# Chunk totals of decays by small DMAs, odd positions' sums on VectorE, joined outputs of pair units

## The chip, the cores and the metric

The kernel runs on one core of a Trainium2 chip. The metric is the device time in microseconds of one launch, given as the median of several runs. A core has five engines with a queue of instructions each: TensorE (PE; its weight loads are shown as PEld), VectorE (DVE), ScalarE (ACT), GpSimd (POOL) and SyncE (SP), which here only issues transfers. Each queue is worked off in its order; engines wait for each other through semaphores. Matmuls write PSUM, eight banks of 128 partitions x 512 f32; everything else works on SBUF, 128 partitions wide.

## What is computed

A recurrent attention with decays, then a feed-forward block (FFN) with exact gelu over its output. There are 4 sequences of 768 tokens, 8 heads of 48; the FFN goes from 384 to 2048 and back.

```python
    f = 1.0 / (1.0 + np.exp(-f_logit))
    for t in range(S):
        state = f[:, :, t, :, None] * state + np.einsum('bhd,bhe->bhde', k[:, :, t], v[:, :, t])
        y[:, :, t] = np.einsum('bhd,bhde->bhe', q[:, :, t], state)
    ...
    x = np.ascontiguousarray(attn_out.transpose(0, 2, 1, 3)).reshape(B * S, H * D)
    h = x @ w_in
    g = 0.5 * h * (1.0 + erf(h * inv_sqrt2))
    return (g @ w_out).astype(np.float32)
```

## The kernel before

**Chunks and units.** The 3072 tokens are cut into 24 chunks of 128, six to a sequence, and two chunks make a unit: units 0 to 11. Inside a chunk the recurrence becomes matrix products: with the running sums g of the log decays, k is scaled by exp(-g) (tile `rg`), q by exp(g) (tile `gt`); scores are masked and applied to v, and a state is carried from chunk to chunk. The state has two heads per matrix, so a chunk has four head pairs (`P2`).

**Pair units.** Units 0 to 4 (`PAIRS`) load two neighbouring tokens into one partition. The 256 tokens of such a unit are split by even and odd position j, and each tile's partitions 0 to 63 are the first chunk, 64 to 127 the second. The other units (natural ones) have one chunk per tile.

**Decays.** `decays(u)` takes the log of the forget gates in two ScalarE operations (E at line 478, L at 481: tile `lf`, bf16). A triangular matmul sums them over the tokens: line 494 for a natural chunk; lines 499 and 500 for each position of a pair unit, even and odd. The sums land in a PSUM bank. Two exponentials on ScalarE make `rg` (509) and `gt` (511). The chunk's total decay, which the state needs with the head dimension on the partitions rather than along the row, comes from narrow matmuls with `lf` as the stationary operand: four of one column for a natural chunk (496, against `negcol`), eight of two columns for a pair unit (504, against `negp`), followed by a small exponential into `gl` (514 or 518). Line 524 scales k and q into `sc`; line 529 casts v.

**Scores and state.** `turn` transposes `sc` into `kq`, for units 0 to 3 by TensorE (557, 563), from unit 4 on by a DMA transpose on SP's queue (545). Scores are matmuls (661 natural, 723 pair) masked by VectorE (570). `carry` adds the chunk's outer product to the state (`rr`, 594) and multiplies by the total decay (`tn`, POOL at 596; for the first chunk of a sequence VectorE at 590), then casts the state to bf16 (`sb`, 601). `gl` is read at 590 and 596 only.

**Outputs.** A natural chunk's output is one TensorE run: `inter` (638, with the state) and the products with v (697). In a pair unit the run is split: `intra` (765, in the array's 64-row form, operation `YI`) for both chunks, and for each chunk a separate operation `YX` with the state (`interp`, 644, in a 64-column form). `outputs` copies the result to `yb` (614) and turns it into `xT`, by TensorE in units 0 to 4 (630, 633), by a DMA transpose from unit 5 (618).

**FFN.** A group of two chunks has eight runs of six matmuls, F1 (801), a gelu each (811), and per chunk four runs of four matmuls, F2 (820). The result is copied to `osb` (834) and stored by SP (836). The last chunk's copy is split in halves between ScalarE and VectorE (827), each half stored from the queue of its own (829).

**What sets the order.** `Plan` holds every operation with an estimated duration, what it reads and writes, buffers from small pools (`slots`) and a priority. `Plan.run` places them one by one, always the one that could start earliest, by priority among near ties; the result is each engine's queue, SP's and POOL's included. Priorities get a random term: one draw for all (`SEED`) and one per unit (`SEEDS`), half-width 0.5, 1, 3 or 8 by the seed modulo 4. ScalarE's tables for exponentials and gelu exclude each other; line 865 loads a table where the order changes from one to the other. While TensorE would stand idle in the first 30 us, junk matmuls (859) are put in.

**Loads.** SP issues the loads of f, k, q and v (433 pair units, 441 natural ones) in a fixed order as buffers come free; POOL issues the weights' (445, 448). SP's one queue also holds the DMA transposes and the stores; an instruction there that waits holds back all behind it.

Of the kernel before, what the change touches and what calls it, by code (L numbers as in the profile page):

```python
# [9 lines left out]
F32 = mybir.dt.float32  # L10
BF16 = mybir.dt.bfloat16
AF = mybir.ActivationFunctionType
# [15 lines left out]
SEEDS = [0, 684, 383, 3363, 2427, 131, 74, 3619, 3555, 1021, 519, 3174]  # L28
# [53 lines left out]
class Plan:  # L82
# [30 lines left out]
    def run(self):  # L113
# [4 lines left out]
        for o in self.ops:  # L118
            if o.prio > -5:
                k = min(max(int(o.prio % 1000) // 20, 0), len(SEEDS) - 1)  # L120
                o.prio += rng.uniform(-SPREAD, SPREAD)
                if SEEDS[k]:
                    w = (0.5, 1.0, 3.0, 8.0)[SEEDS[k] % 4]
                    o.prio += own[k].uniform(-w, w)
        act, switched, mode = None, 0.0, 0
# [79 lines left out]

SIZES = [2, 2, 2, 2, 2, 2, 2, 2, 2, 2, 2, 2]
PAIRS = [0, 1, 2, 3, 4]
WIN = [1024, 512, 512]
EG = [0, 1]
# [14 lines left out]
NGT = 4  # L224
WARM = 30.0
# [5 lines left out]
def kernel(  # L231
# [54 lines left out]
    s_gl = slots(6, [C, 2, P2], F32, "gl")  # L286
    s_kq = slots(3, [C, 2, P2, 2, C], BF16, "kq")
# [53 lines left out]
    for i in range(3):  # L341
        P.add("DVE", 0.2, lambda i=i: nc.vector.memset(
            s_sb.tiles[i].rearrange("p a b -> p (a b)").bitcast(F32), 0.0), wr=[f"sbz{i}"], prio=-70)
    z_lf = [f"lfz{i}" for i in range(3)]
# [106 lines left out]
    def decays(u):  # L451
# [32 lines left out]
        gps = [(s_fh if u in EG else s_m).new() for _ in range(2)]  # L484
        for j, n in enumerate(ns):
            y = X[n]
            gt, rg = s_gt.new(), s_rg.new()
            y.update(sc=s_sc.new(), vb=s_vb.new())
            pr = 20 * u + 10 * j

            def cum(j=j, g=gps[j]):
                g = g.t()
                if not pair:
                    nc.tensor.matmul(g[:, 0:HD], trin, lf.t()[:, j, :, 0:D], start=True, stop=True)  # L494
                    for p in range(P2):
                        nc.tensor.matmul(g[:, HD + p:HD + p + 1], lf.t()[:, j, 2 * p:2 * p + 2, :], negcol,  # L496
                                         start=True, stop=True, skip_group_check=True)
                    return
                nc.tensor.matmul(g[:, 0:HD], trip[:, 0, :], lf.t()[:, 0, :, 0:D], start=True, stop=False)
                nc.tensor.matmul(g[:, 0:HD], trip[:, 1 - j, :], lf.t()[:, 1, :, 0:D], start=False, stop=True)  # L500
                if j:
                    for i in range(2):
                        for p in range(P2):
                            nc.tensor.matmul(g[:, HD + 2 * p:HD + 2 * p + 2], lf.t()[:, i, 2 * p:2 * p + 2, :], negp,  # L504
                                             start=False, stop=(i == 1), skip_group_check=True)
            P.add("PE", (0.54 if j else 0.33) if pair else 0.27, cum,
                  rd=([("lf", u, 0), ("lf", u, 1), "trip", "negp"] if pair else [("lf", u, j), "trin", "negcol"]), wr=[("g", n)],
                  bufs=[lf, gps[j], gt, rg, y["sc"], gl], prio=pr, opens=gps[j], name=f"C{n}")
            P.add("ACT", 0.40, lambda g=gps[j], rg=rg: nc.scalar.activation(rg.t(), g.t()[:, 0:HD], AF.Exp, scale=-1.0),  # L509
                  rd=[("g", n)], wr=[("rg", n)], bufs=[gps[j], rg], table="exp", prio=pr, name=f"RG{n}")  # L510
            P.add("ACT", 0.40, lambda g=gps[j], gt=gt: nc.scalar.activation(gt.t(), g.t()[:, 0:HD], AF.Exp),  # L511
                  rd=[("g", n)], wr=[("gt", n)], bufs=[gps[j], gt], table="exp", prio=pr + 1, name=f"GT{n}")
            if not pair:
                P.add("ACT", 0.19, lambda g=gps[j], j=j: nc.scalar.activation(
                    gl.t()[:, j, :], g.t()[:, HD:HD + P2], AF.Exp),
                    rd=[("g", n)], wr=[("gl", n)], bufs=[gl, gps[j]], table="exp", prio=pr + 2, name=f"GL{n}")
            elif j:
                P.add("ACT", 0.19, lambda g=gps[j]: nc.scalar.activation(
                    gl.t(), g.t()[:, HD:HD + 2 * P2].rearrange("a (p c) -> a c p", c=2), AF.Exp),
                    rd=[("g", n)], wr=[("gl", n - 1), ("gl", n)], bufs=[gl, gps[j]], table="exp", prio=pr + 2,  # L520
                    name=f"GL{n}")
            for w, nm, a, b, off in ((0, "kp", "kt", rg, 0), (1, "qp", "qt", gt, 1)):
                pl = n in (GKP, GQP)[w]
                P.add("POOL" if pl else "DVE", 0.80 if pl else 0.475, lambda w=w, a=a, b=b, y=y, j=j, pl=pl: (nc.gpsimd if pl else nc.vector).tensor_tensor(  # L524
                    y["sc"].t()[:, w, :, 0:D], half(u, x[a], j), b.t().rearrange("p (h d) -> p h d", h=H), ALU.mult),
                    rd=[("gt" if w else "rg", n), (a, n)] + z_sc, wr=[(nm, n)], bufs=[y["sc"], x[a], b], prio=pr + off,
                    port=True, name=f"{nm.upper()}{n}")
            hv = u in HVC
            P.add("ACT" if hv else "POOL", 0.40 if hv else 0.47, lambda y=y, j=j, hv=hv: (nc.scalar.copy if hv else nc.gpsimd.tensor_copy)(  # L529
                y["vb"].t().rearrange("p (h d) -> p h d", h=H), half(u, x["vt"], j)),  # L530
                rd=[("vt", n)], wr=[("vb", n)], bufs=[y["vb"], x["vt"]], prio=pr, name=f"VC{n}")
# [173 lines left out]
    def attn_pair(u):  # L705
# [52 lines left out]
        def intra():  # L758
            for hh in range(2):
# [9 lines left out]
        P.add("PE", 0.5, intra, mode=1, rd=[("am", u, a, b) for a in range(2) for b in range(2)] + [("vb", n) for n in ns],  # L769
              wr=[("yi", n) for n in ns] + ([("yp", n0)] if osb is None else []), bufs=yps + vbs + sum(ams, []) + [U[u]["yb"]],  # L770
              prio=pr + PRI["Y"], opens=yps[0], name=f"YI{u}")
        for cc, n in enumerate(ns):
# [9 lines left out]
    def ffn_group(g):  # L782
# [31 lines left out]
        for s_ in range(s):  # L814
# [9 lines left out]
            if n == NCH - 1:  # L824
                for i, eng in enumerate(("ACT", "DVE")):
                    h = slice(i * d_model // 2, (i + 1) * d_model // 2)
                    P.add(eng, 0.27, lambda h=h, i=i, op=op, osb=osb: copier(not i)(osb.t()[:, h], op.t()[:, h]),
                          rd=[("o", n)], wr=[("os", n, i)], bufs=[op, osb], prio=pr - 1000, name=f"O{n}")
                    P.add("DMA", 0.3, lambda h=h, i=i, n=n, osb=osb: (nc.sync if i else nc.scalar).dma_start(
                        out=out[n * C:(n + 1) * C, h], in_=osb.t()[:, h]), rd=[("os", n, i)], bufs=[osb], prio=-5, lag=4.0,  # L830
# [5 lines left out]
            P.add("DMA", 0.6, lambda n=n, osb=osb: nc.sync.dma_start(out=out[n * C:(n + 1) * C, :], in_=osb.t()),  # L836
                  rd=[("os", n)], bufs=[osb], prio=-5, lag=4.0, name=f"st{n}")
# [61 lines left out]
```

## Time and profile before

| what | us |
|---|---|
| median of 3 runs (182.9 to 183.64) | 183.18 |
| the profiled execution's own time | 183.82 |
| its span, first to last instruction | 181.7 |
| TensorE busy before 27.3 us | 22.9 |
| FFN matmuls on the chain (801 and 820) | 65% of the span |
| small exponentials `gl` (514: 14 x 0.189; 518: 5 x 0.197) | 3.4 |
| VectorE product of k with `rg` (524), one | 0.62 |
| POOL state product (596), one | 0.87 |
| table loads on ScalarE (865), 15 of 1.28 | 19.2 |
| store of the last half tile, issue to landing | 1.6 |

The profile shows one execution. A row of a group names the line, engine, operation, what it writes and reads, the count, then busy time and the mean of one in ns, then the engine's idle time just before such instructions and what ended it. The chain of waits is followed back from the last instruction, at each step to what released it or to the instruction before it on its engine. Times in the text are counted from the span's start.

### The profile page before, as it was taken

The numbers are of one execution on the slowest core, as the hardware profiler recorded it, in microseconds if no ns is written. First come the engines' busy times: TensorE is split into PE (matmuls) and PEld (weight loads), VectorE is DVE, ScalarE is ACT, GpSimd is POOL, SyncE is SP. The second block draws the span as 40 slices with busy tenths as digits, with TensorE's granted clock in tenths as the row PEclk, the third lists the DMA queues.
The fourth block names the chain that finished last, engine by engine and source line by source line (L and its number), as shares of the span: only waits on it lengthen the run. The fifth ranks groups of instructions, "written<-read, shape, count | busy, mean of one in ns | idle before, by whom it ended". The sixth has DMA issues, their size and how long they took to land.

```text
span 181.7 us, 4908 instructions
## 1 busy us (share of the span) xinstructions
PE 173.0 (95%) x1991; PEld 131.9 (73%) x1991; DVE 95.7 (53%) x185; ACT 126.2 (69%) x215; POOL 52.9 (29%) x116
## 2 busy tenths in 40 slices
PE   7889789999999999999999999999999999999992
PEld 2356579866778977669679689966696966887960
DVE  4289730058898650689277770627785217171020
ACT  2775098964986899989957689787483697360900
POOL 7757870003054721050352014014353112100000
PEclk9999999999999999999999999999999999999998
DMA  6999999989999999899999999889999943702112
GB/s 152 261 261 223 266 162 205 201 208 273 269 211 232 184 226 185 183 177 215 191 199 221 152 183 241 168 174 157 216 231 147 220 73 83 209 4 43 43 50 80
DMA packets 106934, 32.61 MB, mean 180 GB/s; under 512 B 102049, under 2 KB 106017, under 8 KB 106913
## 3 DMA queue, kind: packets, MB, share of 16 engines
q1 hardware_dynamic: 104992, 29.07, 77.5%
q0 software_dynamic: 1776, 3.15, 9.9%
q8 instruction: 15, 0.25, 0.6%
q10 hardware_dynamic: 144, 0.10, 0.2%
q14 instruction: 7, 0.05, 0.1%
HBM read 25.17 MB, written 4.72 MB: 165 GB/s over the span
## 4 chain that ended last, share of the span: by engine, by line
PE 79%; DMA 8%; SPq 6%; ACT 2%; DVE 2%; issue 1%; DVEq 0%; ACTq 0%
PE ps L801 33%; PE ps L820 32%; DMA fl<-in_f_logit_dram 6%; SPq L433 6%; DMA xT<-yb 2%; PE ps L661 2%; PE ps L697 2%; PE ps L494 1%; PE ps L638 1%; PE ps L684 1%; PE ps L723 1%; PE ps L557 1%; PE ps L765 1%; PE ps L745 1%; PE ps L644 1%
## 5 line engine op out<-in xcount | busy, mean ns | idle before, releaser
L811 ACT ACTIVATE gT<-ps 128x512 bf16<-128x512 f32 x96 | 58.4, 668 | 23.4 <-PE ps L801 21.8
L801 PE MATMUL ps<-xT,win 128*128 128x256 bf16 x576 | 68.6, 273 | 1.0 <-DMA win<-in_moe_w_in_dram 0.7
L820 PE MATMUL ps<-wout,gT 128*128 128x384 bf16 x384 | 68.3, 326 | 0.0
L801 PEld LDWEIGHTS <-win 128*128 128x128 bf16 x576 | 61.3, 114 | 3.5 <-DMA win<-in_moe_w_in_dram 1.0
L820 PEld LDWEIGHTS <-gT 128*128 128x128 bf16 x384 | 35.9, 98 | 20.9
L524 DVE TENSOR_TENSOR sc<-kt,rg 128x384 bf16<-128x384 f32 x23 | 14.1, 616 | 28.8 <-ACT rg L509 28.7
L596 POOL TENSOR_TENSOR tn<-rr,gl 128x384 f32<-128x384 f32 x16 | 13.9, 870 | 43.1 <-DVE rr L594 23.3
L529 POOL CAST vb<-vt 128x384 bf16<-128x384 f32 x22 | 12.3, 572 | 43.6 <-DMA vt<-in_v_dram 43.4
L570 DVE TENSOR_TENSOR am<-ps,mask 128x512 bf16<-128x512 f32 x28 | 17.5, 683 | 12.3 <-PE ps L661 12.3
L834 DVE COPY osb<-ps 128x384 f32<-128x384 f32 x20 | 11.1, 555 | 23.7 <-PE ps L820 17.6
L865 ACT ACT_TABLE_LOAD x15 | 19.2, 1283 | 0.3
L601 POOL CAST sb<-tn 48x192 bf16<-48x192 f32 x40 | 14.6, 364 | 12.1 <-DVE tn L590 6.5
L614 DVE CAST yb<-ps 128x384 bf16<-128x384 f32 x22 | 12.0, 555 | 8.2 <-PE ps L697 4.3
L478 ACT ACTIVATE fl<-fl 128x768 f32<-128x768 f32 x12 | 10.2, 854 | 8.3 <-DMA fl<-in_f_logit_dram 8.2
L509 ACT ACTIVATE rg<-ps 128x384 f32<-128x384 f32 x24 | 12.0, 502 | 5.4 <-PE ps L496 4.7
L511 ACT ACTIVATE gt<-ps 128x384 f32<-128x384 f32 x24 | 11.8, 499 | 4.2 <-PE ps L504 2.3
L524 DVE TENSOR_TENSOR sc<-qt,gt 128x384 bf16<-128x384 f32 x23 | 13.6, 598 | 1.2 <-ACT gt L511 0.9
L570 DVE TENSOR_TENSOR am<-ps,maskp 128x512 bf16<-128x512 f32 x20 | 12.5, 683 | 2.2 <-PE ps L723 2.1
L859 PE MATMUL ps<-junk 128*128 128x512 bf16 (+2 forms) x35 | 10.6, 437 | 1.8 <-POOL junk L851 1.3
L481 ACT ACTIVATE lf<-fl 128x768 bf16<-128x768 f32 x12 | 10.1, 844 | 0.4
L594 DVE TENSOR_TENSOR rr<-ps,tn 128x384 f32<-128x384 f32 x16 | 8.8, 552 | 1.4 <-POOL tn L596 0.5
L859 PEld LDWEIGHTS <-junk 128*128 128x128 bf16 x35 | 3.6, 113 | 5.9 <-issue 3.3
(68 smaller groups left out, 125.4 us busy)
## 6 DMA issues: line engine op xcount, KB each, us to landing
out_dram<-osb SPq DMA_DIRECT2D x23, 192.0 KB, 2.3
fl<-in_f_logit_dram SPq DMA_DIRECT2D x14, 192.0 KB, 3.9
kt<-in_k_dram SPq DMA_DIRECT2D x14, 192.0 KB, 4.0
qt<-in_q_dram SPq DMA_DIRECT2D x14, 192.0 KB, 3.8
vt<-in_v_dram SPq DMA_DIRECT2D x14, 192.0 KB, 3.5
fl<-in_f_logit_dram SPq DMA_DIRECT2D x5, 384.0 KB, 5.5
kt<-in_k_dram SPq DMA_DIRECT2D x5, 384.0 KB, 5.7
vt<-in_v_dram SPq DMA_DIRECT2D x5, 384.0 KB, 6.4
```

The source lines that it names most:

```text
L509: P.add("ACT", 0.40, lambda g=gps[j], rg=rg: nc.scalar.activation(rg.t(), g.t()[:, 0:HD], AF.Exp, scale=-1.0), rd=[("g", n)], wr=[("rg", n ...
L524: P.add("POOL" if pl else "DVE", 0.80 if pl else 0.475, lambda w=w, a=a, b=b, y=y, j=j, pl=pl: (nc.gpsimd if pl else nc.vector).tensor_tensor(
L529: P.add("ACT" if hv else "POOL", 0.40 if hv else 0.47, lambda y=y, j=j, hv=hv: (nc.scalar.copy if hv else nc.gpsimd.tensor_copy)(y["vb"].t ...
L570: P.add("POOL" if pl else "DVE", 1.15 if pl else 0.61, lambda hh=hh, pl=pl: (nc.gpsimd if pl else nc.vector).tensor_tensor(ams[hh].t(), ap ...
L596: P.add("POOL", 0.83, lambda: nc.gpsimd.tensor_tensor(tn.t(), rr.t(), glb(), ALU.mult), rd=[("rr", n), ("gl", n)], wr=[("tn", n)], bufs=[r ...
L601: P.add("POOL", 0.36, lambda hh=hh: nc.gpsimd.tensor_copy(sb.t()[64 * hh:64 * hh + D, :, D * hh:D * hh + D], tn.t()[64 * hh:64 * hh + D, : ...
L614: P.add("ACT" if help_ else "DVE", 0.40 if help_ else 0.475, lambda: copier(help_)(yb.t()[:, i, :], yp.t()[:, 0:HD]), rd=[("yp", n)], wr=[ ...
L801: nc.tensor.matmul(hps.t()[:, i * tok:(i + 1) * tok].rearrange("a (s t) -> a s t", s=s), col(fo)[:, kk, :], xT.t()[:, :, kk, :], start=(kk ...
L811: nc.scalar.activation(to, fr, AF.Gelu)
L820: nc.tensor.matmul(op.t()[:, 0:d_model], gT.t()[:, fo, s_ * C:(s_ + 1) * C], wout[fo // 4][:, fo % 4, :], start=(fo == 0), stop=(fo == FO ...
L859: nc.tensor.matmul(o.opens.t()[:, 0:w], junk[:, 0:C], junk[:, 0:w], start=True, stop=True, skip_group_check=True)
L865: nc.scalar.preload_act_table_set({"exp": "natural_log_exp_and_others", "gelu": "gelu_and_others"}[o.table])
```

## The change

It has five parts.

1. In units 2 to 11 (`GLD`) the chunk total is no longer computed by narrow matmuls. `gt` of the chunk's last token is already the exponential of the total, one row of 384 numbers. A DMA on SP's queue for each half of the heads (operation `GD`) takes that row (63 and 127 in a pair unit, 127 in a natural one) and writes it over 48 partitions of `gl`, four numbers each. To make these four lie together in the row, `gt` is written in the order half, dimension, pair, so the exponential writes and VectorE's product reads it with a step of four f32. The last chunk of each sequence gets no total, since no state follows. `gl` tiles are set to 1 at the start by VectorE, as the DMA leaves some partitions unwritten.
2. In units 2, 3 and 4 (`G1D`) the odd position's sums aren't matmuls: VectorE subtracts `lf` of the odd position from the even position's sums, into a new SBUF tile `g1`, and ScalarE's exponentials read that.
3. In units 2, 3 and 4 (`YJ`) `intra` and the `interp` runs are one operation, which waits for all that they waited for.
4. The last output tile's halves get an `osb` each. The stores of chunks 16 to 19 (`ROWS`) are issued as two of 64 rows.
5. All `SEEDS` but the first are new. `NUDGE` and `XA` are empty and change nothing.

```diff
-SEEDS = [0, 684, 383, 3363, 2427, 131, 74, 3619, 3555, 1021, 519, 3174]
+SEEDS = [0, 964, 3831, 71, 2582, 463, 2215, 3987, 1759, 51, 1270, 966]
...
+GLD = [2, 3, 4, 5, 6, 7, 8, 9, 10, 11]
+G1D = [2, 3, 4]
+YJ = [2, 3, 4]
+ROWS = [16, 17, 18, 19]
...
+    s_g1 = slots(2 if G1D else 1, [C, HD], F32, "g1")
...
+    for i in range(6):
+        P.add("DVE", 0.07, lambda i=i: nc.vector.memset(s_gl.tiles[i], 1.0), wr=[f"glz{i}"], prio=-60)
...
-        gps = [(s_fh if u in EG else s_m).new() for _ in range(2)]
+        g1d, gld = pair and u in G1D, u in GLD
+        last = 2 * u + 1 if (2 * u + 1) % nC == nC - 1 else None
+        gps = [(s_fh if u in EG else s_m).new() for _ in range(1 if g1d else 2)]
+        if g1d:
+            gps.append(s_g1.new())
...
-                    for p in range(P2):
+                    for p in range(0 if gld or n == last else P2):
                         nc.tensor.matmul(g[:, HD + p:HD + p + 1], lf.t()[:, j, 2 * p:2 * p + 2, :], negcol,
                                          start=True, stop=True, skip_group_check=True)
...
-                if j:
-                    for i in range(2):
-                        for p in range(P2):
-                            nc.tensor.matmul(g[:, HD + 2 * p:HD + 2 * p + 2], lf.t()[:, i, 2 * p:2 * p + 2, :], negp,
-                                             start=False, stop=(i == 1), skip_group_check=True)
...
+                if j == (0 if g1d else 1) and not gld:
+                    sums(g)
...
+            if j and g1d:
+                P.add("DVE", 0.475, lambda a=gps[0], b=gps[1]: nc.vector.tensor_tensor(
+                    b.t().rearrange("p (h d) -> p h d", h=H), a.t()[:, 0:HD].rearrange("p (h d) -> p h d", h=H),
+                    lf.t()[:, 1, :, 0:D], ALU.subtract),
+                    rd=[("g", ns[0]), ("lf", u, 1)], wr=[("g", n)], bufs=[lf, gps[0], gps[1], gt, rg, y["sc"]], prio=pr, name=f"G{n}")
...
+            def gtv(gt=gt):
+                if gld:
+                    return gt.t().rearrange("q (h d p) -> q p h d", h=2, d=D)
+                return gt.t().rearrange("q (p h d) -> q p h d", h=2, d=D)
+            P.add("ACT", 0.40, lambda g=gps[j], gtv=gtv: nc.scalar.activation(
+                gtv(), g.t()[:, 0:HD].rearrange("q (p h d) -> q p h d", h=2, d=D), AF.Exp),
...
+            if gld:
+                def row(r, c, gt=gt):
+                    for hh in range(2):
+                        nc.sync.dma_start(
+                            out=gl.t()[64 * hh:64 * hh + D, c, :],
+                            in_=gt.t()[r:r + 1, :].rearrange("o (h d p) -> o h d p", h=2, d=D)[:, hh])
+                for c, r in (((0, 63), (1, 127)) if pair else ((j, 127),)):
+                    if (pair and not j) or ns[c] == last:
+                        continue
+                    P.add("DMA", 0.15, lambda r=r, c=c, row=row: row(r, c), rd=[("gt", n)] + z_gl, wr=[("gl", ns[c])],
+                          bufs=[gt, gl], prio=-6.5, lag=1.7, lat=0.4, name=f"GD{ns[c]}")
...
+        if u in YJ:
+            olds = [(cc, o) for cc, o in enumerate((osb, mid)) if o is not None]
+
+            def joint():
+                intra()
+                for cc, o in olds:
+                    interp(yps[cc], kq, cc, o)
+            P.add("PE", 0.5 + 0.2 * len(olds), joint, mode=1,
+                  rd=rdi + [("kq", m) for m in ns] + [("sb", ns[cc] - 1, i) for cc, _ in olds for i in range(2)],
+                  wr=[("yp", n) for n in ns], bufs=bfi + [kq] + [o for _, o in olds], prio=pr + PRI["Y"], opens=yps[0], name=f"YI{u}")
...
+                osbs = (osb, s_os.new())
                 for i, eng in enumerate(("ACT", "DVE")):
...
+            def store(n=n, osb=osb):
+                w = C // 2 if n in ROWS else C
+                for r in range(0, C, w):
+                    nc.sync.dma_start(out=out[n * C + r:n * C + r + w, :], in_=osb.t()[r:r + w, :])
```

## The prediction

> **What bounds the kernel now.** I read the page's busy line first, then the chain that ended last, then the chain in order of time, then the busy time by stretches, and last the groups and DMA issues that the change touches.
>
> ```profile
> span 181.7 us, 4908 instructions
> PE 173.0 (95%) x1991; PEld 131.9 (73%) x1991; DVE 95.7 (53%) x185; ACT 126.2 (69%) x215; POOL 52.9 (29%) x116
> PE 79%; DMA 8%; SPq 6%; ACT 2%; DVE 2%; issue 1%; DVEq 0%; ACTq 0%
> ```
>
> TensorE is on the chain for 79% of the span. The busy time by stretches puts all its slack ahead of 27.3 us; from there to 178.1 it is idle about 0.7 us in all. In that stretch an instruction taken from TensorE's queue is time taken from the end, as long as the next one is ready.
>
> ```profile
> 44.04 0.16 PE ps L499
> 44.20 0.16 PE ps L500
> 44.36 0.18 PE ps L504 x8
> 44.54 0.18 PE ps L499
> 44.72 0.16 PE ps L500
> ...
> 122.58 0.16 PE ps L494
> 122.75 0.08 PE ps L496 x4
> ...
> 178.12 0.33 ACT osb L827
> 178.47 0.36 DVE osb L827
> ```
>
> This is the chain in order of time: start, length, what. It prices the sums: 0.18 us for eight narrow matmuls of a pair unit (L504), 0.16 to 0.18 for each wide one (L499, L500), 0.08 for the four of a later chunk (L496). The last two lines show the final output tile: VectorE's half starts only when ScalarE's has ended, though it waits for the same matmul.
>
> ```profile
> 42.00:46.00 4.00, 4.00 (x60) 2.54 (x60) 3.47 (x7) 1.74 (x6) 0.98 (x3) 1.00 1.19 279
> 46.00:50.00 4.00, 4.00 (x81) 3.05 (x80) 3.22 (x8) 3.79 (x7) 0.04 (x1) 1.00 1.16 268
> 50.00:54.00 4.00, 4.00 (x65) 3.00 (x63) 3.95 (x8) 3.31 (x8) 2.47 (x4) 1.00 0.94 213
> 54.00:58.00 4.00, 4.00 (x93) 3.28 (x92) 3.42 (x6) 3.31 (x5) 1.27 (x3) 1.00 1.02 231
> ```
>
> These are stretches of 4 us; after the length come PE, weight loads, DVE, ACT and POOL, then clock, DMA share and GB/s. TensorE is full, but VectorE is busy 14.06 of 16 us too: the pair units' stage has two near-bounds, and VectorE has only 1.94 us to give.
>
> ```profile
> L511 ACT ACTIVATE gt<-ps 128x384 f32<-128x384 f32 x24 | 11.8, 499 | 4.2 <-PE ps L504 2.3 <-PE ps L496 1.9
> L524 DVE TENSOR_TENSOR sc<-qt,gt 128x384 bf16<-128x384 f32 x23 | 13.6, 598 | 1.2 <-ACT gt L511 0.9 <-DMA qt<-in_q_dram 0.4
> L514 ACT ACTIVATE gl<-ps 128x4 f32<-128x4 f32 x14 | 2.4, 189 | 0.0
> kt<-in_k_dram SPq DMA_DIRECT2D x14, 192.0 KB, 4.0
> kq<-sc SPq DMA_TRANSPOSE x16, 3.3
> ```
>
> The first two get a strided gt. The third is what the small DMAs replace, and the last two show what a DMA on SP's queue takes to land here: 3.3 to 4.0 us, among loads that keep the queues' share near 1.0 until 146 us.
>
> **What the Trainium skill says.** TensorEngine Tiling (Array Packing), Instruction Overhead: a matmul with one column costs as much as one of some sixty. The trace agrees in kind: 20 ns a piece at one column (0.08/4), 25 at 48 (L697, 0.20/8). The same page, Key Properties: changing the tiling mode drains TensorE. The trace agrees: four transposes after a 64-column run take 0.33 us, elsewhere 0.22. DMA: Bandwidth & Descriptors, Queues, rings and completion order: each ring is consumed in its order, so a small transfer stands behind loads issued before it. No run yet shows a small one; the 3.3 to 4.0 us above are the nearest. SBUF — State Buffer, Door 1: The DMA port swizzle, says that SBUF has 16-byte lines and that accesses going to another line each time pay; a step of four f32 is just that case. The trace has no such f32 access.
>
> **The change part by part.**
>
> *Narrow matmuls.* Removed in units 2 to 11. Unit 2's run at 25 us, where TensorE isn't the bound: nothing. Units 3 and 4: 2 x 0.18 = 0.36 us. The fourteen later chunks: 14 x 0.081 = 1.14. Units 0 and 1 keep theirs.
>
> *Odd positions' sums by VectorE.* Two wide matmuls go from units 2, 3 and 4; unit 2 again lies ahead of the bound. Units 3 and 4: 0.34 + 0.32 = 0.66 us. Each puts one subtraction on VectorE; the nearest row, a 128x384 tensor op, takes 0.55 to 0.56. Unit 2's falls into VectorE's 12 us of idleness before 38 us. The other two add 1.12 us to 42 to 58 us. The odd position's exponentials wait one VectorE turn longer; behind them on ScalarE is the next unit's work, and the FFN's backlog covers TensorE.
>
> *Outputs in one run.* In unit 2 the order was L765, L644 (0.29), transposes (0.33), L644 (0.29), transposes (0.33). Joined, L644's sixteen take 0.46 as in unit 4 (65.58 us), and the second transposes 0.22: 0.29+0.29-0.46+0.11 = 0.23. Unit 3 loses one break, 0.10. Unit 4 was joined already. Sum 0.33. The price is that the whole run waits for the state of the first chunk.
>
> *Totals by DMA.* ScalarE loses fourteen of 0.189 and three of 0.197 (3.2 us); ScalarE is not on the chain except at the start. SP gains 32 issues (16 totals, two halves each; the last chunk of a sequence has none) at 0.37 to 0.57 us, 12 to 18 us in all, and four more stores. Behind each in SP's queue stand loads and transposes, but SP already stands waiting for the transposes' inputs, which come after gt. What is late is gl: by some 3.5 us. In the stage after 66 us this has room: chunk 12's state is ready at 81.7 us and read at 98.3; chunk 18's at 126.7 and 134.9; chunk 22's at 155.2 and 161.9, the tightest seen about 6 us. In unit 2 it doesn't: gt ends at 39.1, plus issue and 4 us gives 43.3 against 41.5 now, the state moves from 43.1 to 45, and the joined run stood at 46.1. With the 6.4 us that a 384 KB load took there, 1.0 us of TensorE would be lost; at best nothing. I take 0.2.
>
> *Strided gt.* The nearest row is the gelu of pair units, which writes with a step of two: 0.756 us against 0.597 without. Scaled to 384 elements that is +0.12 us on ScalarE, x20 = 2.4, less than the 3.2 it loses. Bounds: nothing, or the streaming part twice (+0.32 on ScalarE, +0.40 on VectorE's read of gt). For VectorE I take +0.1: four such reads in 42 to 58 us, 0.4. With the two subtractions 1.52 of the 1.94 idle us are taken. They won't fit without gaps, so I book a third of it as lost, 0.5.
>
> *Last tile.* With a tile for each half, VectorE copies from 178.12 instead of 178.47: 0.35. The zeroing of gl lies before the first data, free.
>
> *New seeds.* They redraw the order of all units but the first. TensorE has almost no gaps to fill, so a redraw gains little after 27 us; ahead of it there is one: the first twelve F1 matmuls are done by 22.5, but ScalarE takes unit 2's exponentials first and loads the gelu table at 24.5, so a draw could give up to 2.5 us, or take some. I take zero.
>
> Sum: 0.36 + 1.14 + 0.66 + 0.33 + 0.35 = 2.84 off, 0.2 + 0.5 back: 2.14. On the profiled execution, 183.82 us with its span of 181.7 and 2.1 around it, that is 181.7. The runs' median is 183.18, 0.6 lower; carried over, 183.18 - 2.14 = 181.0.
>
> **The rivals.**
>
> *R1, VectorE takes the pair stage's gain.* For it: 88% busy there. Against: some of its work, such as output copies, can be put off to 58 to 74 us, where it is busy 6.3 of 16. Only the later chunks' 1.14 and the tail's 0.35 remain, less 0.3 of gaps: 1.2, time 182.0.
>
> *R2, loads set the pace.* For it: DMA share near 1.0 until 146 us, so what TensorE saves before is waited for again. Against: SP's issues from 83 us on mostly take 0.57 us, not the 1.0 to 1.7 of the crowded start, so the rings have room, and no matmul waits for a load after 27 us. Only the tail's 0.35 stays: 182.8.
>
> *R3, slower: the step of 16 bytes.* If it costs VectorE the full 0.40 us, 42 to 58 us get 1.12 + 1.6 = 2.7 us of VectorE work against 1.94 of idleness, and the idle pieces do not lie where they are needed: all 2.7 are lost. ScalarE, 15.1 of 16 us busy from 66 to 82, gets six exponentials at +0.32 and loses six small ones: +0.8. Against them stand 1.14 + 0.35: +2.0, so 185.2. It decides from about +0.2 us per read on, where 1.12 + 0.8 fill the idle time.
>
> *R4, a lucky opening:* gelu's table first, another 2 us: 179.0.
>
> **How the numbers follow.** Forecast 0.46 (own range 179.6 to 182.0), R1 0.15, R2 0.12, R3 0.19, R4 0.08. The 80% range runs from 179.0, which takes in half of R4, to 184.4, which takes in R1, R2 and the near part of R3. About 0.5% (0.9 us) is what a measurement can tell from no change: the forecast, R4 and two thirds of R1 lie beyond it, 0.63; R2 and the rest of R1 with a sliver of the forecast within, 0.16; R3 and a little of R2 beyond on the other side, 0.21.
>
> **What would show it.** Right: no narrow matmul after unit 1, TensorE's busy time after the start down by about 2.5 us with its idle time still under 1.5; both copies of the last tile starting together; gt's exponential at 0.50 to 0.65 us, VectorE's product with it under 0.75; the small DMAs landing within 4 us. Wrong: the product at 0.9 or above (R3), gaps in TensorE between 42 and 60 us ended by VectorE (R1) or by loads after 66 us (R2), or a long wait of POOL's state product for a DMA with TensorE standing behind it; a start of the dense run at another time than 27.3 us would be R4 or its reverse.

## The result

The changed kernel takes 196.16 us (median of 6 runs, 195.49 to 197.2) where the kernel before takes 183.23 (182.9 to 183.64): a ratio of 1.071, 95% interval 1.0675 to 1.0745. 181.0 was forecast, with a range up to 184.4; the time lies outside it and on the other side. Two runs further down, one of e6 and one of e8, lay over 1.5% above the fastest of the same kernel and are left out of the figures.

The page of the changed kernel, those lines that answer to the ones of before. The DMA line gives the busy share of the 16 DMA engines in tenths, in 40 slices of 4.9 us; the last one is the chain of waits by engine.

```profile
span 194.3 us, 4787 instructions
PE 176.5 (91%) x1907; PEld 129.7 (67%) x1907; DVE 103.3 (53%) x194; ACT 131.2 (68%) x198; POOL 52.6 (27%) x116
...
DMA  6999999959767999844996699887998688762102
...
PE 42%; ACT 18%; DMA 17%; DVE 9%; SPq 6%; issue 5%; POOL 1%; DVEq 0%; ACTq 0%; POOLq 0%
```

TensorE has 84 matmuls fewer, and its part of the chain fell from 79% to 42%. What took its place on the chain is DMA, ScalarE and VectorE. Before, the DMA engines too hardly stood still until the loads were over:

```profile
DMA  6999999989999999899999999889999943702112
```

That line of the kernel before shows eights and nines from 5 us to 146 us. In the changed kernel the line has holes of 4 to 7 from 39 us on, and the loads go on until about 166 us. The busy time by stretches, first before, then after (length, PE, weight loads, DVE, ACT, POOL, clock, DMA share, GB/s):

```profile
27.30:66.00 38.70, 38.57 (x562) 31.24 (x561) 22.48 (x42) 31.19 (x53) 10.21 (x20) 1.00 1.04 224
66.00:120.00 54.00, 53.82 (x570) 42.73 (x569) 31.10 (x57) 45.08 (x77) 12.77 (x25) 1.00 0.99 193
```

```profile
27.30:66.00 38.70, 35.42 (x441) 26.88 (x440) 22.80 (x39) 29.13 (x45) 9.88 (x18) 1.00 0.89 182
66.00:120.00 54.00, 49.17 (x522) 37.24 (x522) 28.24 (x48) 41.85 (x59) 11.54 (x22) 0.97 0.85 171
```

TensorE is idle 3.3 and 4.8 us in them, where it was idle 0.1 and 0.2, and every other engine but VectorE in the first stretch is less busy as well. No engine became the bound: all of them got their data late. In time order, the chain has steps like these:

```profile
63.44 4.10 DMA kq<-sc
67.58 0.64 PE ps L775 x32
...
77.90 3.10 DMA kt<-in_k_dram
...
190.97 0.33 ACT osb L893
191.32 0.36 DVE osb L893
```

What SyncE did ahead of the first of them, from the timeline of its queue (start, length, line, what, how many):

```profile
50.38 2.41 SPq L553 DMA_DIRECT2D gl<-gt  x4
52.90 1.00 SPq L905 DMA_DIRECT2D out_dram<-osb  x2
53.95 1.72 SPq L455 DMA_DIRECT2D fl<-in_f_logit_dram  x1
55.76 0.53 SPq L905 DMA_DIRECT2D out_dram<-osb  x1
56.39 0.39 SPq L455 DMA_DIRECT2D kt<-in_k_dram  x1
56.87 2.55 SPq L553 DMA_DIRECT2D gl<-gt  x4
59.53 1.33 SPq L597 DMA_TRANSPOSE kq<-sc  x1
60.91 0.57 SPq L905 DMA_DIRECT2D out_dram<-osb  x1
61.58 1.11 SPq L455 DMA_DIRECT2D qt<-in_q_dram  x1
62.74 0.58 SPq L455 DMA_DIRECT2D vt<-in_v_dram  x1
63.44 1.77 SPq L597 DMA_TRANSPOSE kq<-sc  x1
```

In the first 10.5 us of this list the queue has issued eight small DMAs, which took 5.0 us, and two loads. Nowhere does it stand still for long; it is full. The transposes of `sc` that TensorE waits for at 63.44 us stand in it like the loads: VectorE's last product for them was done by 59.9 us, and the second transpose was issued 3.6 us later, behind a store and two loads. The rows of the strided tile, by tile (count, then min/median/max in ns, first and last start; the last line gives issue to landing of the small DMAs):

```profile
L547 ACT ACTIVATE gt<-ps x21: 479/876/957, 7.4 to 166.3; 128x384 f32<-128x384 f32 x21
...
L553 SPq DMA_DIRECT2D gl<-gt x32: 501/582/2326, 39.8 to 166.7; - x32
...
DMA to landing us min/median/max: 1.7/1.9/4.1
```

The exponential takes 876 ns with the step, 0.50 us without. A small DMA of 48 pieces of 16 bytes takes 582 ns to issue and lands soon after.

### The profile page after: what moved, and what is told of

The parts are those of the page before. It is cut to its first block, busy times and chain, and to the rows that moved or that the text cites. A ratio compares the mean times of both kernels' runs of the same rounds, so it can differ in the third digit from the quotient of the medians.

```text
span 194.3 us, 4787 instructions
## 1 busy us (share of the span) xinstructions
PE 176.5 (91%) x1907; PEld 129.7 (67%) x1907; DVE 103.3 (53%) x194; ACT 131.2 (68%) x198; POOL 52.6 (27%) x116
## 4 chain that ended last, share of the span: by engine, by line
PE 42%; ACT 18%; DMA 17%; DVE 9%; SPq 6%; issue 5%; POOL 1%; DVEq 0%; ACTq 0%; POOLq 0%
PE ps L885 20%; PE ps L866 16%; ACT gT L876 7%; DMA fl<-in_f_logit_dram 6%; SPq L447 5%; DMA kq<-sc 5%; ACT gt L547 5%; DVE sc L574 4%; ACT L934 3%; DMA kt<-in_k_dram 2%; DMA vt<-in_v_dram 2%; DMA xT<-yb 1%; ACT fl L492 1%; DVE am L622 1%; DMA gl<-gt 1%
## 5 line engine op out<-in xcount | busy, mean ns | idle before, releaser
L876 ACT ACTIVATE gT<-ps 128x512 bf16<-128x512 f32 x96 | 57.8, 670 | 26.6 <-PE ps L866 25.0
L866 PE MATMUL ps<-xT,win 128*128 128x256 bf16 x576 | 70.7, 277 | 2.5 <-DMA xT<-yb 1.0
L866 PEld LDWEIGHTS <-win 128*128 128x128 bf16 x576 | 62.0, 115 | 6.7 <-DMA xT<-yb 1.3
L574 DVE TENSOR_TENSOR sc<-kt,rg 128x384 bf16<-128x384 f32 x23 | 14.6, 640 | 22.0 <-ACT rg L541 21.9
L900 DVE COPY osb<-ps 128x384 f32<-128x384 f32 x20 | 11.1, 554 | 21.0 <-PE ps L885 20.4
L574 DVE TENSOR_TENSOR sc<-qt,gt 128x384 bf16<-128x384 f32 x23 | 19.7, 871 | 4.6 <-ACT gt L547 4.4
L653 POOL CAST sb<-tn 48x192 bf16<-48x192 f32 x40 | 13.9, 347 | 14.5 <-DVE tn L642 12.4
L547 ACT ACTIVATE gt<-ps 128x384 f32<-128x384 f32 x21 | 16.4, 815 | 2.0 <-PE ps L519 2.0
L666 DVE CAST yb<-ps 128x384 bf16<-128x384 f32 x22 | 11.7, 552 | 10.8 <-PE ps L696 5.5
L541 ACT ACTIVATE rg<-ps 128x384 f32<-128x384 f32 x21 | 10.5, 512 | 5.5 <-PE ps L525 4.1
L928 PE MATMUL ps<-junk 128*128 128x512 bf16 (+3 forms) x37 | 11.2, 434 | 2.1 <-POOL junk L920 1.3
L495 ACT ACTIVATE lf<-fl 128x768 bf16<-128x768 f32 x12 | 10.1, 845 | 0.4
```

What stands on the lines that cost most here:

```text
L547: P.add("ACT", 0.40, lambda g=gps[j], gtv=gtv: nc.scalar.activation(gtv(), g.t()[:, 0:HD].rearrange("q (p h d) -> q p h d", h=2, d=D), AF. ...
L653: P.add("POOL", 0.36, lambda hh=hh: nc.gpsimd.tensor_copy(sb.t()[64 * hh:64 * hh + D, :, D * hh:D * hh + D], tn.t()[64 * hh:64 * hh + D, : ...
L866: nc.tensor.matmul(hps.t()[:, i * tok:(i + 1) * tok].rearrange("a (s t) -> a s t", s=s), col(fo)[:, kk, :], xT.t()[:, :, kk, :], start=(kk ...
L876: nc.scalar.activation(to, fr, AF.Gelu)
L928: nc.tensor.matmul(o.opens.t()[:, 0:w], junk[:, 0:C], junk[:, 0:w], start=True, stop=True, skip_group_check=True)
```

## The experiments

Two theories stood at the start: A, the step of 16 bytes (the prediction's R3) slows ScalarE and VectorE; C, the small DMAs do it, by SP's time for issuing them (C1), by waiting for `gt` with loads queued behind (C2), or by `gl` landing late (C3). A third, B, was that the new seeds drew a bad order. In e1 to e9 only what an operation issues was edited, so the order of the queues is that of the changed kernel (in e4 that of the kernel before).

**e1, no step.** The total rows still go through DMAs, in an order that doesn't match the heads; nothing else differs.

```diff
-                if gld:
-                    return gt.t().rearrange("q (h d p) -> q p h d", h=2, d=D)
                 return gt.t().rearrange("q (p h d) -> q p h d", h=2, d=D)
```

> The kernel after in the same order of instructions, but gt written and read with a step of one; the small DMAs take the same row, so the totals that they carry belong to other dimensions than they should (the state's decays are changed). Theory A, the step of 16 bytes is the loss (one gt exponential 0.88 instead of 0.50, one product 0.87 instead of 0.55, 20 chunks): 182 to 186 us. Theory B, the new order by itself is bad: 191 to 196. Theory C, the small DMAs hold up SP's queue and the state: 191 to 196.

193.21 us, 1.0521 (1.05 to 1.0541). Its page:

```profile
L545 ACT ACTIVATE gt<-ps 128x384 f32<-128x384 f32 x21 | 10.1, 498 | 1.9 <-PE ps L519 1.9
L572 DVE TENSOR_TENSOR sc<-qt,gt 128x384 bf16<-128x384 f32 x23 | 13.1, 585 | 2.5 <-ACT gt L545 2.2
```

Both operations are back at their old durations, and only 3.0 of the 12.9 us went.

**e2, step without DMAs; e3, neither.** The totals of units 2 to 11 stay at 1.

```diff
-                    for hh in range(2):
+                    for hh in range(0):
```

> The kernel after in the same order with the strided gt, without the 32 small DMAs: the totals are left at 1, so the state does not decay between chunks from unit 2 on. Theory A: 192 to 196 us, as after. Theory B: 192 to 196. Theory C: 182 to 188.

> Both edits, in the order of the kernel after: gt with a step of one and no small DMAs (totals left at 1). Theory A: 181 to 185 us, close to the run with the plain gt alone. Theory B: 190 to 196 still. Theory C: 181 to 185, with all of the gain from the DMAs. If A and C share it, this run is lower than either edit alone by about the sum of both gains.

e2: 187.41, 1.0222 (1.0206 to 1.0237). e3: 181.98, 0.9921 (0.9907 to 0.9936). With e1 and the changed kernel this is a square: the DMAs cost 8.8 us beside the step (196.2 - 187.4) and 11.2 without it (193.2 - 182.0); the step costs 3.0 beside the DMAs and 5.4 without them. Together they make 14.2. What is left without them beats the kernel before, but its totals are missing; e13 below has them.

**e4, the step alone in the kernel before,** units 2 to 11; VectorE's product reads `gt` through the same `gtv`.

```diff
-            P.add("ACT", 0.40, lambda g=gps[j], gt=gt: nc.scalar.activation(gt.t(), g.t()[:, 0:HD], AF.Exp),
+            def gtv(gt=gt):
+                if u >= 2:
+                    return gt.t().rearrange("q (h d p) -> q p h d", h=2, d=D)
+                return gt.t().rearrange("q (p h d) -> q p h d", h=2, d=D)
+            P.add("ACT", 0.40, lambda g=gps[j], gtv=gtv: nc.scalar.activation(
+                gtv(), g.t()[:, 0:HD].rearrange("q (p h d) -> q p h d", h=2, d=D), AF.Exp),
...
```

> The kernel before in its own order with one edit: gt of units 2 to 11 is written and read with a step of four f32. Theory A: +0.38 us in 20 exponentials and +0.32 us in 20 products, in stages where ScalarE or VectorE is nearly full: 188 to 194 us. Theory B and theory C: below 185 us.

186.66, 1.0173 (1.0155 to 1.0192): +3.2 us, in the direction of A, but below the 188 to 194 that A called for.

**e5 and e6, what of the DMA hurts.** From e1: in e5 the DMAs write spare tiles that nobody reads (totals stay 1), in e6 they read a constant tile of ones and don't wait for `gt`.

```diff
-                            out=gl.t()[64 * hh:64 * hh + D, c, :],
+                            out=spare[gl.slot][64 * hh:64 * hh + D, c, :],
```

```diff
-                            in_=gt.t()[r:r + 1, :].rearrange("o (h d p) -> o h d p", h=2, d=D)[:, hh])
+                            in_=still[r:r + 1, :].rearrange("o (h d p) -> o h d p", h=2, d=D)[:, hh])
```

> As the run with the plain gt (193.2 us), but the 32 small DMAs write spare tiles that nobody reads, and the totals stay at 1: SP waits for gt and issues as before, and the state waits for no landing. Theory C1, SP's time for the issues and the in-flight window of its DMAs is the loss: 190 to 194. Theory C2, SP standing in wait for gt with loads and transposes behind it: 190 to 194. Theory C3, the state waits for the landing: 182 to 185.

> As the run with the plain gt, but the 32 small DMAs read a constant tile (totals 1), so SP needn't wait for gt; issues and the state's wait for the landing stay. C1: 188 to 194. C2: 182 to 186. C3: 185 to 193, since the landings come a little earlier only.

e5: 194.87, 1.0634 (1.0561 to 1.0707); C3 falls. e6: 191.1 (190.25 to 192.86), 1.0436 (1.0364 to 1.0508), against 193.21 for e1; C2 is at most a small part.

**e7, one DMA of each two; e8, all from POOL's queue; e9, one larger DMA instead of two.** e7 and e8 start from e1 (in e7 the second half's totals stay 1), e9 from the changed kernel: its `gt` row is padded to 512, and one DMA writes all 128 partitions.

```diff
-                    for hh in range(2):
-                        nc.sync.dma_start(
+                    for hh in range(1):
+                        nc.sync.dma_start(
```

```diff
-                        nc.sync.dma_start(
+                        nc.gpsimd.dma_start(
```

```diff
-                    for hh in range(2):
-                        nc.sync.dma_start(
-                            out=gl.t()[64 * hh:64 * hh + D, c, :],
-                            in_=gt.t()[r:r + 1, :].rearrange("o (h d p) -> o h d p", h=2, d=D)[:, hh])
+                    nc.sync.dma_start(out=gl.t()[:, c, :], in_=gt.t()[r:r + 1, :].rearrange("o (d p) -> o d p", p=P2))
```

> As the run with the plain gt, but only one of the two small DMAs of each total is issued (16 in place of 32; the other half of the heads keeps 1). C1: the loss of 11.2 us is halved, 186 to 189. C2 and C3: 191 to 193, as the wait for gt and for the landing stays.

> As the run with the plain gt, but the 32 small DMAs are issued from POOL's queue at the same place of the order; SP has none of them. C1 and C2: SP is free, 182 to 187, the more of it lost the longer POOL stands for gt and for its issues. C3: 190 to 196, the landing is later still.

> The kernel after in the same order, with gt rows padded to 512 so that one DMA over 128 partitions carries a total: 16 issues in place of 32, 2 KB each in place of twice 0.8 KB; the step of four stays. If SP's time for issues is the loss: two thirds of the 8.8 us that the DMAs cost beside the strided gt come back, 189 to 192 us. If it is the traffic, the wait for gt or for the landing: 194 to 197.

e7: 185.98, 1.0131 (1.0097 to 1.0165): 7.2 of the 11.2 us go with half of the DMAs. e8: 188.22 (186.04 to 188.6), 1.023 (1.0155 to 1.0304): with SP relieved, some 5 of the 11.2 us come back, less than expected. e9: 188.78, 1.0309 (1.0292 to 1.0326): it moves more bytes with half of the issues, and of the DMAs' 8.8 us 1.4 stay (188.8 - 187.4). It is the number of issues that counts and not the bytes, and more than in proportion.

**e10 and e11, the order drawn anew.** e10 takes the totals back to TensorE for all units; e11 gives the planner measured durations (VectorE's product too: 0.79 for 0.475).

```diff
-GLD = [2, 3, 4, 5, 6, 7, 8, 9, 10, 11]
+GLD = []
```

```diff
-            P.add("ACT", 0.40, lambda g=gps[j], gtv=gtv: nc.scalar.activation(
+            P.add("ACT", 0.78 if gld else 0.40, lambda g=gps[j], gtv=gtv: nc.scalar.activation(
...
-                    P.add("DMA", 0.15, lambda r=r, c=c, row=row: row(r, c), rd=[("gt", n)] + z_gl, wr=[("gl", ns[c])],
+                    P.add("DMA", 1.17, lambda r=r, c=c, row=row: row(r, c), rd=[("gt", n)] + z_gl, wr=[("gl", ns[c])],
```

> The kernel after without its first part (GLD empty): totals by narrow matmuls again, gt with a step of one; the odd positions' sums by VectorE, the joined outputs, the split stores and the new seeds stay, the planner orders anew. If the small DMAs and the step were all of the loss: 182 to 185 us. If the new seeds or the other parts cost as well: above 186.

> The kernel after with the planner's prices set to what was measured: 1.17 us for a total's two issues in place of 0.15, 0.78 for the strided exponential in place of 0.40, 0.79 for the product in place of 0.475; the planner orders anew. If the order made with wrong prices is a main part of the loss: 184 to 190. If SP and ScalarE just have the time to give in no order: 193 to 198.

e10: 191.93, 1.0486 (1.0429 to 1.0544). e11: 212.98, 1.1635 (1.1592 to 1.1678). e10 fell on the side that spoke for a loss by the seeds or the other parts, e11 outside both ranges. Neither tells anything of the DMAs: the planner draws another order for other operations or prices. e13 has the same work as e10, in the order of the changed kernel, and is 8.4 us faster; so much can a drawn order be worth, and so a part is tested by editing what an operation issues.

**e12, before without the totals' work in units 2 to 11** (they stay 1); **e13, the changed kernel's order with the totals computed as before;** **e14, before without the totals that nobody reads,** in the last chunk of three sequences.

```diff
-                    for p in range(P2):
+                    for p in range(0):
...
-                    for i in range(2):
+                    for i in range(0 if u >= 2 else 2):
```

```diff
-                    for p in range(0 if gld or n == last else P2):
+                    for p in range(0 if n == last else P2):
...
-                if j == (0 if g1d else 1) and not gld:
+                if j == (0 if g1d else 1):
                     sums(g)
...
+                if gld and not pair and n != last:
+                    nc.scalar.activation(gl.t()[:, j, :], g.t()[:, HD:HD + P2], AF.Exp)
```

```diff
-                    for p in range(P2):
+                    for p in range(0 if n % nC == nC - 1 else P2):
```

In all three the small exponentials go or come with the matmuls; e13 has neither the step nor the DMAs.

> The kernel before in its own order without the narrow matmuls and the small exponentials of units 2 to 11 (totals left at 1 there): what removing them can give at most, with nothing put in their place. By the prediction's sum 1.14 + 0.36 = 1.5 us: 181.5 to 182.2. If TensorE is not the bound in those places: 182.8 to 183.5.

> The kernel after in its own order of instructions, with the totals by narrow matmuls and small exponentials again (put back into the same places), gt with a step of one and no small DMAs. If the first part is all of the loss: 182.0, as with totals left out, plus what the totals cost (1.5 by the prediction's sum, 2.75 by the run of before without them): 183.5 to 184.8 us. If the other parts or the order lose as well: above 186.

> The kernel before in its own order, without the totals of the last natural chunk of each of three sequences, which no state needs: twelve narrow matmuls and three small exponentials less. A seventh of what all totals gave (2.75 us for 17 exponentials): 0.3 to 0.5 us below before. If TensorE only counts by chance: no change.

e12: 180.51, 0.9855 (0.9826 to 0.9884): in this order 2.75 us are all that any cheaper way to the totals can bring. e13: 183.55, 1.0005 (0.9991 to 1.002): the other four parts together are worth nothing that shows, and the first one makes all of the loss. e14: 183.28, 0.9993 (0.9978 to 1.0008).

**e15, the DMAs alone.** The kernel before, its order and all its work, with 32 small DMAs put into SP's queue behind `gt`'s exponentials. They copy a constant into spare tiles: they wait for nothing of the kernel, and nothing waits for them.

```diff
...
+                    for hh in range(2):
+                        nc.sync.dma_start(out=spare[gl.slot][64 * hh:64 * hh + D, j, :],
+                                          in_=still[127:128, :].rearrange("o (h d p) -> o h d p", h=2, d=D)[:, hh])
```

> The kernel before in its own order, all of its work kept, plus 32 small DMAs on SP's queue after the gt exponentials, from a constant tile into spare tiles that nobody reads. If SP's time for issues is the loss (32 x 0.58 us), whatever the order: +6 to +12 us. If the loss needed the order of the kernel after, the wait for gt or the landing: less than +3.

194.59, 1.0619 (1.0586 to 1.0653): +11.1 us, as much as in the other order. Its stretches and its DMAs:

```profile
27.30:66.00 38.70, 38.20 (x557) 30.91 (x555) 22.64 (x42) 30.62 (x52) 9.86 (x19) 1.00 0.99 204
66.00:120.00 54.00, 48.94 (x480) 37.49 (x477) 27.32 (x51) 39.68 (x68) 12.91 (x25) 0.94 0.89 171
```

```profile
L517 SPq DMA_DIRECT2D spare<-still x32: 507/590/1731, 34.1 to 157.3; - x32
...
DMA to landing us min/median/max: 1.7/2.9/5.2
```

The middle stretch is that of the changed kernel again: 49 of 54 us for TensorE, a DMA share of 0.89 (0.85 there). The transfers' own traffic is small: 1536 packets of 16 bytes at some 8 ns are 12.8 us over 16 engines, 0.8 us. (Part of these 5 us stands beside a clock of 0.94, so idle time and clock aren't told apart there.)

**e16 to e18, SP's time or something else of a DMA.** Open was whether it is SP's time that sends the loads out late, or the completion semaphores: in the records SP's DMAs take eight of them in turn, so each could have to wait until the eighth before it has landed. e16 replaces each idle DMA by eight instructions that only pass time on SP (16 of them take 0.9 us in its records); e17 issues the idle DMAs from ScalarE; e18 makes each 2 KB over 128 partitions.

```diff
-                        nc.sync.dma_start(out=spare[gl.slot][64 * hh:64 * hh + D, j, :],
-                                          in_=still[127:128, :].rearrange("o (h d p) -> o h d p", h=2, d=D)[:, hh])
+                        for i in range(8):
+                            nc.sync.drain()
```

```diff
-                        nc.sync.dma_start(out=spare[gl.slot][64 * hh:64 * hh + D, j, :],
+                        nc.scalar.dma_start(out=spare[gl.slot][64 * hh:64 * hh + D, j, :],
```

```diff
-                        nc.sync.dma_start(out=spare[gl.slot][64 * hh:64 * hh + D, j, :],
-                                          in_=still[127:128, :].rearrange("o (h d p) -> o h d p", h=2, d=D)[:, hh])
+                        nc.sync.dma_start(out=spare[gl.slot][:, j, :],
+                                          in_=still[127:128, :].rearrange("o (d p) -> o d p", p=P2))
```

> The kernel before with its own order and all its work; in place of each of the 32 idle DMAs of e15 stand eight instructions on SP that drain its queue and move no data. Issue theory (SP's time alone displaces the loads): the loss grows with the time that they take on SP; at some 0.07 us each, 0.55 us in place of a DMA's 0.58, it is 8 to 11 us as in e15; if they take half as long, 2 to 5. Window theory (each DMA takes one of eight completion semaphores, and the loads wait for those): no DMA is added, so 0 to 1 us slower than before, whatever time they take on SP.

> The kernel before with its own order and all its work; the 32 idle DMAs of e15 are issued by ScalarE instead of SP. Issue theory: SP has its time back, ScalarE has [...] room for part of it: 0 to 5 us slower than before. Window theory: the DMAs still take their places among the completion semaphores, which SP and ScalarE share, and the loads wait as in e15: 8 to 11 us slower.

> As e15 (the order and the work of before, with 32 idle DMAs on SP), but each DMA writes all 128 partitions, 2 KB, instead of 48 partitions. If a fixed cost of each DMA on its queue makes the loss: 10 to 12 us slower than before, as e15 with its 11.1. If it is the form of the piece of 48 partitions: 2 to 6 us, in proportion to e9's 1.4 us for 16 of the larger ones. If the number of partitions counts (128 against 48): 15 us or more.

e16: 187.31 (186.01 to 188.33), 1.0193 (1.0125 to 1.026). e17: 188.97, 1.0276 (1.0229 to 1.0324). e18: 222.24, 1.2118 (1.2081 to 1.2154). e16's +3.6 us are more, and e17's +5.3 less, than the semaphores called for (0 to 1, and 8 to 11). e18 doesn't tell what it was meant for: the two DMAs of a pair write the same place, so the second waits on SP until the first has landed. One pair in the timeline of its SP queue:

```profile
55.54 4.93 SPq L517 DMA_DIRECT2D spare<-still  x2
```

where a pair mostly took 1.2 to 1.5 us in e15. But it adds a third amount of SP's time. Summed from the records of SP's queue, from 27.3 us to the end of the last load's issue (a pause is a stretch of over 0.15 us between the end of one issue and the start of the next; e18's exclude those inside the pairs):

| | until the last load | issues of loads, stores, transposes | pauses | what was added | last load later by | time, against before |
|---|---|---|---|---|---|---|
| before | 118.0 | 92.1 | 20.4 | | | |
| e16 | 120.8 | 87.9 | 11.1 | some 13 | 2.8 | +3.6 |
| e15 | 129.3 | 88.9 | 8.9 | some 24 | 11.3 | +11.1 |
| e18 | 159.5 | 88.5 | 12.2 | some 52, waits with it | 41.5 | +38.6 |

The time follows the last load's issue each time, and what was added exceeds the delay by 10, 13 and 10 us. So SP's queue had some 10 to 13 us to give; what was taken beyond that came back at the end nearly in full. The slack has two parts. The other issues get shorter by 3 to 4 us: in before, a load's issue after a pause (there are three) takes 0.37 us in the median and 0.70 otherwise; in e15 one behind a small DMA (nine) takes 0.58. The rest comes out of the pauses. Some 6 to 7 us of these lie ahead of the first addition, at 34 us, in every run; behind it they fall from 13.6 us to 2.6 in e15: the queue is full. The semaphores aren't it: in the records of e15 each of SP's DMAs after 27 us is issued at least 1.9 us after the eighth before it has landed. And e7 fits. In the order of the changed kernel the slack was some 6 us: against e3, e7 adds 9.5 us and its last load comes 3.6 us later, e1 adds 19.8 and comes 13.6 later. With the step it was some 10: against e2 the changed kernel adds 20.1 and comes 9.6 later.

e17 shows that another queue isn't free either. ScalarE spends 19.5 us on the 32 issues. SP's other issues take 92.8 us, hardly more than before, but its pauses grow from 20.4 to 25.9 us, and the last load is 5.8 us later. So SP stands waiting for work that comes late, which points to ScalarE's time rather than to slower issues; no run separates it from the transfers themselves. What is left in e8 stays open.

## Why the prediction was wrong

**Totals by DMA: the step that failed.** The prediction had the count right, "32 issues", and a price close to it, "0.37 to 0.57 us, 12 to 18 us in all" (20 us in the changed kernel), and then costed them at nothing, since "SP already stands waiting for the transposes' inputs, which come after gt". That cover was named and not counted. The sum it needed was to be had from the trace of before: from 39.8 us, just behind unit 2's `gt`, to the end of the last load's issue at 145.3 us, SP's pauses add up to 10.8 us, in sixteen pieces. The longest is the one between these two lines:

```profile
73.09 0.67 SPq L441 DMA_DIRECT2D fl<-in_f_logit_dram  x1
75.86 2.66 SPq L545 DMA_TRANSPOSE kq<-sc  x2
```

Against the prediction's own 12 to 18 us that leaves 1 to 7 us over, against the measured 20 some 9. The runs showed that 10 to 13 us can be taken in the order of before, and 6 to 10 in that of the changed kernel; 20 to 24 were. The loss of 8.8 to 11.2 us is this one term.

The Trainium skill, DMA: Bandwidth & Descriptors, Issuing engines are not separate DMA queues, says that the time of a sequencer to start a DMA is usually small relative to the DMA itself. Here it isn't: 0.58 us to issue 0.8 KB that lands 1.9 us after the start of its issue, not much less than the 0.6 to 0.7 us for a load of 192 KB, and in a queue that has no time left it is the issue that is paid for.

**R2 was the nearest rival, and was dismissed by a wrong reading.** "SP's issues from 83 us on mostly take 0.57 us, ... so the rings have room" looked at the length of one issue and not at how many stood in a row. R2 also had no slower side: it asked what TensorE's saved time would gain, not what happens when loads come later than before.

**gl late.** 0.2 us was booked for an arrival of 4 us; the landing took 1.9 us in the median, and e5 shows that the loss is there when nobody waits for it. (In the changed kernel POOL's state product waits 4.9 us in all for `gl`, a mark that the prediction named; it isn't where the loss comes from.) The prediction's own ground for 4 us, that a small transfer stands behind the loads issued before it, isn't borne out by the 1.9 us against 3.6 to 4.0 of the loads.

**Strided gt: a size.** +0.12 us on ScalarE and +0.1 on VectorE were taken, with bounds of +0.32 and +0.40. Measured: +0.38 (0.50 to 0.876), above its bound, and VectorE's product

```profile
L574 DVE TENSOR_TENSOR sc<-qt,gt 128x384 bf16<-128x384 f32 x23 | 19.7, 871 | 4.6 <-ACT gt L547 4.4
```

from 0.55 to 0.87 us in the median (551 to 870 ns), within its bound. R3's mark, "0.9 or above", is nearly met, and its mechanism is real: +3.2 us in e4, +5.4 between e3 and e2, where R3 booked 2.4 for it (1.6 and 0.8). The gelu with a step of two was no guide to a step of four f32. The place that SBUF — State Buffer, Door 1: The DMA port swizzle, gave for a price was right in kind; the size had to be measured.

**Narrow matmuls.** 1.14 + 0.36 us were booked; e12 measures 2.75 for them with their small exponentials, to which the prediction gave nothing. e14 shows that a piece of it need not show: three chunks' totals were expected to bring 0.3 to 0.5 us and brought nothing that shows.

**Odd sums, joined outputs, seeds, last tile.** 0.66 + 0.33 + 0 + 0.35 were booked, less 0.5 of gaps; e13 measures +0.1 (-0.2 to +0.4) for all of them. The last tile is the part that can be seen: its halves still go one after the other, at 190.97 and 191.32 us, though each has its own `osb`. In the built program VectorE's copy waits for ScalarE's all the same; both read the same PSUM tile. The others weren't separated; a loss as in R1, VectorE standing in the way, may be among them.

**What held:** no narrow matmul after unit 1; the subtraction of the odd sums at 0.56 us; landing within 4 us in all but the extreme case of 4.1.

**What didn't:** TensorE's idle time between 27.3 us and its end, to stay "under 1.5", is 10.1 us, and its busy time there, to fall by some 2.5 us, rose from 150.1 to 153.6 with 74 matmuls fewer. A part of that stands beside the clock of 0.97 in the middle stretch; the rest isn't explained.

## What to carry to other kernels

A queue that only issues transfers is an engine with a bound of its own: before anything is moved to it, add up the pauses between its issues, from the first place where something is added to the last load, and compare them with count times price, which here was 0.58 us even for 0.8 KB. Here 10.8 us of pauses stood against 32 x 0.58 = 18.6 us. It is a bound and not a promise: not every pause can be filled. A saving on the bounding engine is worth nothing if it is paid in such a queue: 2.75 us of TensorE's and ScalarE's work were bought with 20 us of SyncE's. And where a planner draws the order, test a part by changing what an operation issues, not what the planner sees; one redraw alone (e10 against e13) was worth 8 us.

## What the runs showed that was not expected

- ScalarE writing 384 f32 at a step of 16 bytes: 0.876 us against 0.50; VectorE reading them: 0.87 against 0.55 (medians). The step costs 0.8 to 1.0 ns per element (0.32 and 0.38 us over 384).
- Small DMAs cost more than in proportion: 16 small DMAs 4.0 us, 32 of them 11.2, since the first come out of the queue's slack.
- Sixteen larger DMAs (128 pieces) were cheaper to issue than the 48-piece ones: 0.49 against 0.58 us.
